# A kernel's first token tile takes its first product in plain float32 from unrounded weights, under a new order of work

## The chip, the cores and the metric

The kernel runs on one core of one Trainium2 chip. The metric is the device time of one execution in microseconds, as the median of several runs.

## The reference

```python
def _attn_ref(r, k, v, w, u):            # r, k, v: (4, 8, 768, 48); w, u: (8, 48)
    ...
    for t in range(S):
        kt, vt, rt = (k[:, :, t], v[:, :, t], r[:, :, t])
        cur = np.einsum('bhd,bhe->bhde', u[None] * kt, vt)
        y[:, :, t] = np.einsum('bhd,bhde->bhe', rt, state + cur)
        state = w[None, :, :, None] * state + np.einsum('bhd,bhe->bhde', kt, vt)

def _moe_ref(x, w_in, w_out, a, b):      # x: (3072, 384), w_in: (384, 2048), w_out: (2048, 384)
    h = x @ w_in
    h2 = h * h
    h3 = h2 * h
    P = a[0] + a[1] * h + a[2] * h2 + a[3] * h3
    Q = 1.0 + np.abs(b[0]) * np.abs(h) + np.abs(b[1]) * h2
    g = P / (Q + 1e-06)
    return (g @ w_out).astype(np.float32)
```

The attention's output y, with its heads side by side, is the x of the second function. The weights w_in and w_out come as float64, all else as float32.

## The kernel before

**Attention.** The 3072 tokens make 24 blocks of 128; the loads (kh, rh, vn) and the matmuls work on blocks or on pairs m of two blocks (12 pairs). For a block, kh and rh are scaled by powers of the decay (L633, L637), r times k is formed for the term in u (L641, into a tile m), multiplied by u (L646), reduced (L651, dt) and multiplied by v (L655). PE transposes kh and rh (tk and tr, L660), copies bring them to SBUF as kt and ys (L549, a helper `copy` that all engines' copies go through), a products (L682) are masked on DVE (L696), kv products (L712) carry the state, which DVE adds into vs (L725) and decays (L745), and y products (L736) give the result, added to m (L741). PE transposes m to x (L753). There are 7 tiles m.

**Two products.** A token tile f is two blocks (256 tokens; 12 tiles). x is copied to its rounded float32r half xth, and a subtraction gives the remainder xtl (L765). The 2048 columns of w_in are 16 groups j of 128. A slice s is two groups of one tile: 8 slices a tile, 97 in all, since the last one is halved. For one slice PE takes the first product f1 (`mm`, L775): for each j three row chunks, each by three float32r products of 256 columns (rounded weight by xth, rounded weight by xtl, remainder of weight by xth). Then the rational function: on ACT L817, L823, L828, L833 (ln, into z) and L837 (exp); on DVE u3 (L841), the rounded half of g (L847), p (L851), d (L857) and the remainder of g (L861, on DVE for slices 0 to 19, on POOL from 20 on). The second product f2 (`mm2`, L779 to L781) takes three float32r products of 384 columns for each j and block.

**Weights.** They come in 28 pieces, 12 of w_in (128x512) and 16 of w_out (128x384), each a float64 read as pairs of integers. A piece is loaded on SP's queue, and then goes from engine to engine: `cv_exp` on ACT (L516), `cv_shift` on DVE (L522), `cv_up` and `cv_sign` on ACT (L503, L507), for every fourth piece `cv_or` on DVE (L535) instead, `cv_round` on POOL (L540). The float32 piece that results (bits) is split: the rounded half (`cv_hi`, L549, on ACT or DVE) and the remainder (`cv_lo`, L546, on DVE or POOL). Four constant tiles keep halves and remainders: wi_hi, wi_lo, wo_hi, wo_lo.

**Order.** The kernel lists its steps as tasks with an engine or a choice of two, a cost, dependencies and buffers. `order_of` is a planner that runs when the kernel is built: it gives each task a key (from the tables AT for the pairs, CT for the pieces, OFF for the kinds of step), places the tasks on engines and returns one list, and the program is emitted in that order. Each engine then works through its own part strictly in order. Between the first rounds of work the planner puts matmuls on constants, called warm (L1096, bf16, 128x128), up to the first f2. After the last slices a flag decides whether a general form of the whole runs; in these runs it does not.

The first product in x and the second are float32r. The attention's products a, kv and y, and `us` (L401: one row of weights by 384 columns, in the preparation of the tables), are plain float32; the trace has two records for one such product.

Of the kernel before, what the change touches and what calls it, by code (L numbers as in the profile page):

```python
# [31 lines left out]
PRM = {'AT': (7.27, 41.94, 71.38, 117.31, 149.61, 223.87, 236.91, 267.74, 286.41, 287.5, 376.53, 394.8),  # L32
# [6 lines left out]
 'DUE': 7.86,  # L39
 'DX': 2.27,  # L40
 'FULL': (),
 'HFREE': 1,
# [4 lines left out]
 'OFF': {'LV': 249.97,
         'Lk': 358.43,
         'Lr': -577.02,
         'Lv': -349.7,  # L50
# [1168 lines left out]
```

## Time and profile before

| | |
|---|---|
| median of three runs | 562.29 us (561.52 to 562.76) |
| the profiled execution | 562.68 us, span 560.9 us |
| PE busy | 533.8 us (95%) |
| DVE busy | 464.8 us (83%) |
| ACT busy | 424.0 us (76%) |
| POOL busy | 267.4 us (48%) |
| mean granted clock of TensorE | 0.99 |

PE is the TensorE's matmul, PEld its weight loads, DVE the VectorE, ACT the ScalarE, POOL the GpSimd and SP the SyncE, whose queue issues the loads. The span is the time from the first to the last instruction of the profile; the execution's own time contains 1.8 us more. A line such as L775 is a line of the kernel, and out<-in are the tiles by name. A word in brackets behind a row of a timeline is the idle time that the engine had ahead of it, and whose work ended that. Durations of matmuls overlap: what one costs is the distance between two starts.

### The profile page before, as it was taken

To read this page: it belongs to the slowest core of one execution; us is meant where nothing else is said; L and a number is where in the kernel's file an instruction comes from. 1 tells how busy PE (TensorE), PEld (TensorE's weight loads), DVE (VectorE), ACT (ScalarE), POOL (GpSimd) and SP (SyncE) were. 2 spreads that over 40 slices of the span, in tenths; PEclk is the share of its full clock that TensorE was granted. 3 is DMA by queue.
4 is the path that set the end of the run, shared out by engine and by line. 5 is a ranking of instruction groups with operands and counts; after the bars stand their busy time and mean duration, and the time that the engine had idled before them with its cause. 6 is when DMAs were issued, how large, how long until landed. Compare 5 with 4: busy or idle time off the path is not lost.

```text
span 560.9 us, 14727 instructions
## 1 busy us (share of the span) xinstructions
PE 533.8 (95%) x5968; PEld 518.2 (92%) x5968; DVE 464.8 (83%) x738; ACT 424.0 (76%) x707; POOL 267.4 (48%) x260
## 2 busy tenths in 40 slices
PE   7899867699999999999999999999999999999996
PEld 6799756699998999988999999999999999999996
DVE  4887999999999776998799989668888977776773
ACT  6759887998776788965766767778878676888781
POOL 6688677671041223795569423327633312223221
PEclk9999979899999999999999999999999999999999
DMA  8556386503200006065133203003300000000001
GB/s 202 168 157 168 115 188 174 135 22 71 57 16 16 2 27 123 5 132 109 28 68 87 41 2 85 16 1 88 63 30 15 1 30 2 0 30 1 30 1 34
DMA packets 100032, 35.64 MB, mean 64 GB/s; under 512 B 93298, under 2 KB 96372, under 8 KB 99956
## 3 DMA queue, kind: packets, MB, share of 16 engines
q1 hardware_dynamic: 99956, 34.62, 25.7%
q8 instruction: 49, 0.80, 0.6%
q14 instruction: 27, 0.22, 0.1%
HBM read 29.89 MB, written 4.72 MB: 62 GB/s over the span
## 4 chain that ended last, share of the span: by engine, by line
PE 71%; DVE 17%; ACT 6%; issue 3%; POOL 2%; DVEq 0%; ACTq 0%; POOLq 0%
PE h L775 30%; PE o L779 10%; PE o L781 10%; PE o L780 10%; PE warm L1096 3%; PE y L736 3%; DVE g L847 2%; DVE q L851 2%; DVE vs L725 2%; DVE ys L696 1%; DVE h L841 1%; PE x L753 1%; DVE ys L549 1%; PE tr L660 1%; DVE h L857 1%
## 5 line engine op out<-in xcount | busy, mean ns | idle before, releaser
L861 POOL TENSOR_TENSOR g<-q,z 128x512 fp32r<-128x512 f32 (+1 forms) x77 | 99.1, 1287 | 188.6 <-DVE q L857 162.1
L775 PE MATMUL h<-xth,wi_hi 128*128 128x256 f32 x576 | 164.1, 285 | 1.8 <-DVE wi_hi L549 1.8
L775 PE MATMUL h<-xth,wi_lo 128*128 128x256 f32 x576 | 161.7, 281 | 0.9 <-POOL wi_lo L546 0.9
L775 PE MATMUL h<-xtl,wi_hi 128*128 128x256 f32 x576 | 161.5, 280 | 0.0
L779 PE MATMUL o<-wo_hi,g 128*128 128x384 f32 x384 | 134.5, 350 | 0.0
L781 PE MATMUL o<-wo_hi,g 128*128 128x384 f32 x384 | 130.4, 340 | 2.1 <-DVE g L861 2.1
L780 PE MATMUL o<-wo_lo,g 128*128 128x384 f32 x384 | 130.1, 339 | 0.0
L817 ACT ACTIVATE q<-h 128x512 f32<-128x512 f32 (+1 forms) x97 | 57.3, 591 | 81.0 <-PE h L775 78.3
L847 DVE SCALAR_TENSOR_TENSOR g<-h,sig,z 128x512 fp32r<-128x512 f32 (+1 forms) x97 | 72.1, 743 | 49.7 <-ACT z L837 46.9
L775 PEld LDWEIGHTS h<-xth,wi_hi 128*128 128x128 f32 x576 | 108.7, 189 | 2.5 <-DVE wi_hi L549 2.0
L775 PEld LDWEIGHTS h<-xth,wi_lo 128*128 128x128 f32 x576 | 108.7, 189 | 1.1 <-POOL wi_lo L546 1.1
L775 PEld LDWEIGHTS h<-xtl,wi_hi 128*128 128x128 f32 x576 | 108.8, 189 | 0.0
L841 DVE SCALAR_TENSOR_TENSOR h<-t,sig,h 128x512 f32<-128x512 f32 (+1 forms) x97 | 72.1, 744 | 7.7 <-ACT t L828 7.1
L851 DVE SCALAR_TENSOR_TENSOR q<-w,sig,g 128x512 f32<-128x512 f32 (+1 forms) x97 | 72.1, 743 | 5.1
L781 PEld LDWEIGHTS o<-wo_hi,g 128*128 128x128 f32 x384 | 72.6, 189 | 3.2 <-DVE g L861 3.2
L823 ACT ACTIVATE w<-q,off,root 128x512 f32<-128x512 f32 (+1 forms) x97 | 75.5, 779 | 0.0
L828 ACT ACTIVATE t<-h,off,root 128x512 f32<-128x512 f32 (+1 forms) x97 | 74.5, 769 | 0.1
L779 PEld LDWEIGHTS o<-wo_hi,g 128*128 128x128 f32 x384 | 72.7, 189 | 0.7
L780 PEld LDWEIGHTS o<-wo_lo,g 128*128 128x128 f32 x384 | 72.7, 189 | 0.0
L837 ACT ACTIVATE z<-z,lnb 128x512 f32<-128x512 f32 (+1 forms) x97 | 69.7, 718 | 2.4
L833 ACT ACTIVATE z<-w,lnb 128x512 f32<-128x512 f32 (+1 forms) x97 | 66.3, 683 | 3.1 <-DVE g L861 0.6
L857 DVE SCALAR_TENSOR_TENSOR q<-h,sig,q 128x512 f32<-128x512 f32 (+1 forms) x77 | 57.1, 741 | 1.9
(275 smaller groups left out, 804.4 us busy)
## 6 DMA issues: line engine op xcount, KB each, us to landing
sti<-in_moe_w_in_dram SPq DMA_DIRECT2D x12, 512.0 KB, 4.6
sto<-in_moe_w_out_dram SPq DMA_DIRECT2D x16, 384.0 KB, 3.4
rh<-in_r_dram SPq DMA_DIRECT2D x24, 192.0 KB, 3.5
vn<-in_v_dram SPq DMA_DIRECT2D x24, 192.0 KB, 3.6
kh<-in_k_dram SPq DMA_DIRECT2D x24, 192.0 KB, 3.3
out_dram<-os SPq DMA_DIRECT2D x24, 192.0 KB, 1.9
vs<-in_v_dram SPq DMA_DIRECT2D x32, 96.0 KB, 3.7
wraw<-in_w_dram SPq DMA_DIRECT2D x1, 1.5 KB, 2.2
```

What stands on the lines that cost most here:

```text
L775: nc.tensor.matmul(o, wt_[:, cc, ts(j, P)], x_[:, cc], start=(n == 0), stop=(n == 3 * NCC - 1))
L779: nc.tensor.matmul(o, hi, wo_hi[:, j], start=first, stop=False)
L780: nc.tensor.matmul(o, hi, wo_lo[:, j], start=False, stop=False)
L781: nc.tensor.matmul(o, lo, wo_hi[:, j], start=False, stop=last)
L823: nc.scalar.activation(g["w"], w_, AF.Square, scale=RB, bias=KB)
L828: nc.scalar.activation(g["t"], g["h"], AF.Square, scale=RA, bias=KA)
L833: nc.scalar.activation(g["z"], g["w"], AF.Ln, scale=2.0 ** -LN_SHIFT, bias=lnb[:, 2:3])
L837: nc.scalar.activation(g["z"], g["z"], AF.Exp, scale=-1.0, bias=lnb[:, 1:2])
L841: nc.vector.scalar_tensor_tensor(g["h"], g["t"], KAP, g["h"], op0=ALU.add, op1=ALU.mult)
L847: nc.vector.scalar_tensor_tensor(g["hi"], g["h"], c0, g["z"], op0=ALU.add, op1=ALU.mult)
L851: nc.vector.scalar_tensor_tensor(g["q"], g.get("w", g["q"]), qe, g["hi"].bitcast(F32), op0=ALU.add, op1=ALU.mult)
L861: e.tensor_mul(g["lo"], g["d"], g["z"])
```

## The change

Three things change together.

**Tile 0 in plain float32.** For the tiles in FULL (only tile 0, slices 0 to 7) f1 is `mm_full`: three plain float32 products for each j, of the unrounded piece f by an unrounded x. 144 float32r products become 48 plain ones. xth of tile 0 is float32, and it has no xtl. The first product of tile 0 depends on the piece's `cv_round` instead of its remainder; halves and remainders of w_in are needed from tile 1 on, and the remainder of a w_in piece is made after the last plain product that reads it.

**Buffers.** The pieces no longer have a place in four constant tiles. f, hi and lo of each are tiles of their own, from two rings ("wi" with 25 tiles, "wo" with 33), in which a piece's remainder takes the place of an f that has served. The z tiles ("tb") go from 3 to 2, since the conversions no longer use them, and the m tiles from 7 to 6.

**The order.** All tables of the planner have new numbers, halves and remainders have a table of their own (CS), and some costs differ. So nearly all steps stand elsewhere.

```diff
- 'FULL': (),
+ 'FULL': (0,),
...
- 'OFF': {'LV': 249.97,
...
+ 'OFF': {'LV': 270.26,
...
-    NM = 7
+    NM = 6
+    NTB = 2
+    NWI = FF // CW * NCC * 2 + 1
+    NWO = NJ * 2 + 1
...
-    wi_hi = cst.tile([P, NCC, FF], F32R, name="wi_hi")
-    wi_lo = cst.tile([P, NCC, FF], F32R, name="wi_lo")
-    wo_hi = cst.tile([P, NJ, DM], F32R, name="wo_hi")
-    wo_lo = cst.tile([P, NJ, DM], F32R, name="wo_lo")
...
+    def win(cc, j):
+        return pieces[(CW // P + NCC) * (j // (CW // P)) + cc], ts(j % (CW // P), P)
...
+    def cv_tile(c, nm, dt):
+        tag, bufs = ("wo", NWO) if c["n"] == DM else ("wi", NWI)
+        c[nm] = cst.tile([P, c["n"]], dt, tag=tag, name=f"w{nm}{c['nm']}", bufs=bufs)
+        return c[nm]
...
     def cv_hi(c, e):
-        copy(e, c["hi"], c["f"])
+        copy(e, cv_tile(c, "hi", F32R), c["f"])
...
-            xts[f] = tuple(at.tile([P, NCC, N1], F32R, tag=s, name=f"{s}{f}") for s in ("xth", "xtl"))
+            xts[f] = tuple(
+                at.tile([P, NCC, N1], F32 if f in FULL else F32R, tag=s, name=f"{s}{f}") for s in (("xth",) if f in FULL else ("xth", "xtl"))
+            )
...
-            for wt_, x_ in ((wi_hi, hi), (wi_hi, lo), (wi_lo, hi)):
-                nc.tensor.matmul(o, wt_[:, cc, ts(j, P)], x_[:, cc], start=(n == 0), stop=(n == 3 * NCC - 1))
+            w_, c = win(cc, j)
+            for nm, x_ in (("hi", hi), ("hi", lo), ("lo", hi)):
+                nc.tensor.matmul(o, w_[nm][:, c], x_[:, cc], start=(n == 0), stop=(n == 3 * NCC - 1))
                 n += 1
 
+    def mm_full(o, j, x_):
+        for cc in range(NCC):
+            w_, c = win(cc, j)
+            nc.tensor.matmul(o, w_["f"][:, c], x_[:, cc], start=(cc == 0), stop=(cc == NCC - 1))
...
-        mm(hps[s][:, ts(jj, N1)], j0 + jj, *xts[f])
+        (mm_full if f in FULL else mm)(hps[s][:, ts(jj, N1)], j0 + jj, *xts[f])
...
-        g["z"] = ew_tile(s, "tb", "z")
+        g["z"] = ew_tile(s, "tb", "z", bufs=NTB)
...
-            add(("co", p), lambda e, c=c, p=p: cv_lo(c, e), t + 3, {"D": 0.07 + 0.53 * x, "G": 0.15 + 1.07 * x}, [("ch", p)], use=[("bits", p)])
+            add(("co", p), lambda e, c=c, p=p: cv_lo(c, e), t + 1, {"D": 0.07 + 0.53 * x, "G": 0.15 + 1.07 * x}, [("ch", p), *last_use(p)], new=[(tag, ("wl", p))], use=[("wf", p)])
...
+            xin, win = ("xh", "cr") if full else ("xl", "co")
...
-                    deps + [("co", p0 + cc) for cc in range(NCC)], new=[] if jj else [("h", h)], use=[("xt", f)] + ([h] if jj else []), cols=2304)
+                    deps + [(win, p0 + cc) for cc in range(NCC)], new=[] if jj else [("h", h)], use=[("xt", f)] + ([h] if jj else []) + used([p0 + cc for cc in range(NCC)], s, full), cols=3072 if full else 2304)
```

Three places of the order follow, before and then now. Behind a name stands the number of the tile that the program gave it: the 0 in h0 is the slice, the 2 in tr2 and kh2 the block, and wfi0_1 is the plain piece f of w_in, column group 0, chunk 1; wloo1 is the remainder of the w_out piece 1.

PE, the first rows of slice 0's first product, before:

```order
L775 MATMUL h0_902<-xth0_825,wi_hi_103 128x256
L775 MATMUL h0_902<-xtl0_826,wi_hi_103 128x256
L775 MATMUL h0_902<-xth0_825,wi_lo_104 128x256
L775 MATMUL h0_902<-xth0_825,wi_hi_103 128x256
L775 MATMUL h0_902<-xtl0_826,wi_hi_103 128x256
L775 MATMUL h0_902<-xth0_825,wi_lo_104 128x256
```

PE, the same place now:

```order
L790 MATMUL h0_851<-xth0_807,wfi0_0_632 128x256
L790 MATMUL h0_851<-xth0_807,wfi0_1_217 128x256
L790 MATMUL h0_851<-xth0_807,wfi0_2_242 128x256
L667 MATMUL tr2_863<-identw_80,rh0_105 112x128 x4
L790 MATMUL h0_851<-xth0_807,wfi0_0_632 128x256
L790 MATMUL h0_851<-xth0_807,wfi0_1_217 128x256
L790 MATMUL h0_851<-xth0_807,wfi0_2_242 128x256
L790 MATMUL h1_882<-xth0_807,wfi0_0_632 128x256
```

Each j was nine products and is three, and the transposes tr2 of the second pair stand between the first j's products.

DVE, around tile 0's copy of x and the first product, before:

```order
L549 CAST xth0_825<-x0_814 128x3x128
L745 TENSOR_TENSOR vs0_107<-vs0_107,w128_93 48x384
L522 TENSOR_SCALAR bitso3_849<-cp6_834 128x384
L765 TENSOR_TENSOR xtl0_826<-x0_814,xth0_825 128x3x128
L765 TENSOR_TENSOR xtl0_826<-x1_843,xth0_825 128x3x128
L522 TENSOR_SCALAR bitsi1_2_918<-cp9_912 128x512
L546 TENSOR_TENSOR wo_lo_106<-bitso9_785,wo_hi_105 128x384
L522 TENSOR_SCALAR bitso4_946<-cp10_929 128x384
L633 TENSOR_TENSOR kh2_113<-kh2_113,wkn_92 128x8x48
L549 COPY kt_114<-tk2_979 112x512
L549 COPY ys0_115<-tr2_1026 48x512
L549 COPY ys1_116<-tr2_1026 48x512
```

DVE, the same place now:

```order
L556 COPY xth0_807<-x1_824 128x3x128
L640 TENSOR_TENSOR kh2_109<-kh2_109,wkn_92 128x8x48
L644 TENSOR_TENSOR rh0_105<-rh0_105,wrn_91 128x8x48
L553 TENSOR_TENSOR wloo1_861<-wfo1_798,whio1_858 128x384
L648 TENSOR_TENSOR m2_868<-rh0_105,kh2_109 128x384
L556 COPY ys0_111<-tr2_863 48x512
L653 TENSOR_TENSOR m2_868<-m2_868,ub_85 128x384
L529 TENSOR_SCALAR wfi3_2_886<-cp23_876 128x512
L658 TENSOR_REDUCE dt2_895<-m2_868 128x8
L662 TENSOR_TENSOR m2_868<-vn2_782,dt2_895 128x384
L856 SCALAR_TENSOR_TENSOR h0_851<-t0_893,sig_100,h0_851 128x512
L529 TENSOR_SCALAR wfo3_909<-cp6_904 128x384
```

The remainders xtl0 are gone, the copies of block 2's transposes stood behind four conversion steps and now stand behind one, and slice 0's u3 (L856 now) comes in the same dozen.

DVE, between the remainder of slice 14 and the steps of slices 15 and 16, before:

```order
L861 TENSOR_TENSOR g14_2468<-h14_2370,z14_2420 128x512
L841 SCALAR_TENSOR_TENSOR h15_2458<-t15_2492,sig_100,h15_2458 128x512
L696 TENSOR_TENSOR ys1_116<-a(3, 1)_2423,mask_81 64x8x64
L847 SCALAR_TENSOR_TENSOR g15_2533<-h15_2458,sig_100,z15_2505 128x512
L851 SCALAR_TENSOR_TENSOR q15_2488<-w15_2502,sig_100,g15_2533 128x512
L857 SCALAR_TENSOR_TENSOR h15_2458<-h15_2458,sig_100,q15_2488 128x512
L741 TENSOR_TENSOR m6_2139<-y6_2538,m6_2139 128x384
L861 TENSOR_TENSOR g15_2533<-h15_2458,z15_2505 128x512
L841 SCALAR_TENSOR_TENSOR h16_2510<-t16_2558,sig_100,h16_2510 128x512
L741 TENSOR_TENSOR m7_2196<-y7_2561,m7_2196 128x384
```

DVE, the same place now:

```order
L732 TENSOR_TENSOR vs0_103<-kv4_0_2415,vs0_103 48x384
L876 TENSOR_TENSOR g14_2404<-h14_2280,z14_2377 128x512
L732 TENSOR_TENSOR vs0_103<-kv4_0_2415,vs0_103 48x384
L732 TENSOR_TENSOR vs0_103<-kv4_1_2416,vs0_103 48x384 x2
L703 TENSOR_TENSOR ys0_111<-a4_0_2450,mask_81 64x8x64 x2
L703 TENSOR_TENSOR ys1_112<-a4_1_2451,mask_81 64x8x64 x2
L658 TENSOR_REDUCE dt10_2548<-m10_2498 128x8
L662 TENSOR_TENSOR m10_2498<-vn10_2256,dt10_2548 128x384
L648 TENSOR_TENSOR m11_2592<-rh1_107,kh2_109 128x384
L748 TENSOR_TENSOR m8_2165<-y8_2553,m8_2165 128x384
L856 SCALAR_TENSOR_TENSOR h15_2506<-t15_2570,sig_100,h15_2506 128x512
L748 TENSOR_TENSOR m9_2293<-y9_2575,m9_2293 128x384
```

Adds, masks and reduces of pairs 4 and 5 stand ahead of slice 15's u3, where one mask stood behind it before.

More of the change, by code (lines that the diff above doesn't have):

```diff
@@ new lines @@
+ 'OFF': {'LV': 270.26,
+         'Lk': 774.15,
+         'Lr': -796.68,
+         'Lv': -312.07,
+         'a': -341.47,
+         'ae': 398.71,
+         'ba': 33.75,
+         'bb': -348.95,
+         'beta': -354.71,
+         'bs': -201.32,
+         'bv': -386.72,
+         'c0': -322.33,
+         'c2': 127.85,
+         'c3': -103.81,
+         'ca': -140.2,
+         'ch': 121.32,
+         'cl': -34.78,
+         'cl_': -128.33,
+         'co': -647.77,
+         'coef': 293.84,
+         'cr': 213.5,
+         'cs': -175.01,
+         'ctr': -337.17,
+         'cu': -134.42,
+         'd': -35.41,
+         'ex': -222.41,
+         'f1': -18.42,
+         'f2': 29.16,
+         'flag': -59.53,
+         'flagm': 645.83,
+         'flagt': 524.35,
+         'hi': 12.18,
+         'id': 91.47,
+         'inv': -624.91,
+         'kv': 150.51,
+         'kve': -232.22,
+         'ln': 63.38,
+         'lo': -1043.9,
+         'msk': 27.33,
+         'od': 129.99,
+         'os': -15.92,
+         'p': 68.22,
+         'pad': 25.39,
+         'pl': 54.79,
+         'pow': -277.52,
+         'q': 362.68,
+         'rest': 10.15,
+         'sk': 150.8,
+         'sq': -301.08,
+         'sr': -807.06,
+         'st0': 436.05,
+         't': 292.34,
+         'tab': -679.44,
+         'tk': 221.19,
+         'tke': 109.8,
+         'tr': -205.98,
+         'tre': 482.82,
+         'turn': -129.33,
+         'u3': -36.29,
+         'ub': 38.7,
+         'ube': -359.69,
+         'ubp': -906.35,
+         'uw': -294.57,
+         'w': -428.73,
+         'w128': -805.12,
+         'wl': 257.36,
+         'wp': 221.72,
+         'x': -170.77,
+         'xh': 511.5,
+         'xl': 55.87,
+         'y': -297.22,
+         'ye': 218.13,
+         'z': 276.11},
@@ L124 @@
  'WARM0': 1.6,
- 'WARM1': 260.37,
- 'X': (49.3, 8.02, 7.96, 3.84)}
+ 'WARM1': 732.75,
+ 'X': (52.55, 30.05, 13.36, 10.85),
+ 'FULL2': (),
+ 'FINE': {}}
 ENGINES = "PDAGS"
@@ L555, in tile_linear_attention_rational_ffn @@
         for cc in range(NCC):
-            piece(wi_hi[:, cc, ts(g, CW)], wi_lo[:, cc, ts(g, CW)], wi32[ts(cc, P), ts(g, 2 * CW)], CW, f"i{g}_{cc}")
+            piece(wi32[ts(cc, P), ts(g, 2 * CW)], CW, f"i{g}_{cc}")
         for j in range(g * (CW // P), (g + 1) * (CW // P)):
-            piece(wo_hi[:, j, :], wo_lo[:, j, :], wo32[ts(j, P), :], DM, f"o{j}")
+            piece(wo32[ts(j, P), :], DM, f"o{j}")
     TR = HALF + D
@@ L888, in f2 @@
             c = ds(jj * N1 + hf * P, P)
+            if f in FULL2:
+                w_, o = wout(j0 + jj), ops[f][hf][:, 0:DM]
+                nc.tensor.matmul(o, gs[s]["hi"][:, c].bitcast(F32), w_["f"], start=opens(s) and jj == 0, stop=False)
+                nc.tensor.matmul(o, gs[s]["lo"][:, c], w_["hi"], start=False, stop=closes(s) and jj == nj - 1)
+                continue
             mm2(
@@ L939, in add, with last_use @@
             tags[buf] = tag
+    def last_use(p):
+        g, k = divmod(p, NCC + CW // P)
+        if k < NCC:
+            us = [("f1", s, jj) for s, (f, j0, nj) in enumerate(SL) for jj in range(nj) if f in FULL and (j0 + jj) // 4 == g]
+        else:
+            us = [("f2", s, 1) for s, (f, j0, nj) in enumerate(SL) if f in FULL2 and j0 <= 4 * g + k - NCC < j0 + nj]
+        return us[-1:]
     def build():
@@ L1008, in build, with used @@
                 add(("xh", n), lambda e, n=n: xt_hi(n, e), due(m) + 13, {"A": 0.37, "D": 0.47}, [("x", n)], use=[("x", n), ("xt", m)])
-                add(("xl", n), lambda e, n=n: xt_lo(n), due(m) + 14, {"D": 0.47}, [("xh", n)], use=[("x", n), ("xt", m), ("m", n)])
-        lastf = {SL[s][0]: s for s in range(NS)}
+                if m not in FULL:
+                    add(("xl", n), lambda e, n=n: xt_lo(n), due(m) + 14, {"D": 0.47}, [("xh", n)], use=[("x", n), ("xt", m), ("m", n)])
+        def used(ps, s, full):
+            return [(nm, p) for p in ps for nm in (("wf",) if full else ())]
+        keep = [(nm, p) for nm in ("wh", "wl") for p in range(len(pieces))]
         for s in range(NS):
```

157 lines of the change are left out of this document (44 added, 113 removed), and 12 rows, old and new, of the table PRM.

## Prediction

> **What bounds the kernel now.** I read the page's head and its chain first, then a table of stretches, then single rows where one engine waits. From the page: the span, the busy line, and the chain that ended last by engine.
>
> ```profile
> span 560.9 us, 14727 instructions
> PE 533.8 (95%) x5968; PEld 518.2 (92%) x5968; DVE 464.8 (83%) x738; ACT 424.0 (76%) x707; POOL 267.4 (48%) x260
> PE 71%; DVE 17%; ACT 6%; issue 3%; POOL 2%; DVEq 0%; ACTq 0%; POOLq 0%
> ```
>
> PE is busy for 95% of the span, but 17% of the chain is DVE. The stretches tell where. Columns: the stretch in us, its length, busy time and instructions of PE, PEld, DVE, ACT and POOL, granted clock, DMA share, GB/s.
>
> ```profile
> core 0: us, PE busy (x) PEld busy (x) DVE busy (x) ACT busy (x) POOL busy (x), PEclk, DMA share, GB/s
> 0.00:17.00 17.00, 13.69 (x159) 12.42 (x160) 8.51 (x18) 12.24 (x24) 9.91 (x25) 1.00 0.87 222
> 17.00:40.00 23.00, 20.67 (x461) 19.67 (x458) 21.86 (x50) 14.74 (x31) 17.69 (x17) 1.00 0.47 135
> 40.00:56.00 16.00, 16.00 (x234) 15.91 (x232) 11.54 (x17) 14.47 (x28) 13.91 (x14) 1.00 0.73 177
> 56.00:117.00 61.00, 47.33 (x619) 42.18 (x617) 58.16 (x97) 51.97 (x96) 42.77 (x41) 0.92 0.56 142
> 117.00:157.30 40.30, 40.27 (x450) 39.22 (x449) 38.36 (x59) 33.14 (x55) 11.44 (x13) 1.00 0.24 50
> 157.30:185.00 27.70, 26.83 (x354) 25.71 (x354) 26.27 (x42) 19.20 (x33) 9.65 (x11) 1.00 0.05 16
> 300.00:549.00 249.00, 248.97 (x2403) 246.10 (x2400) 199.89 (x308) 190.36 (x304) 95.15 (x82) 1.00 0.12 28
> ```
>
> From 117 us on PE has next to no gap (0.03 in 40.3 us, 0.9 in 27.7, 0.03 in 249). Its work there is fixed, so the end moves with the time at which PE becomes full. From 56 to 117 PE is idle for 13.7 us, at a mean granted clock of 0.92, while DVE is idle for only 2.8: tile 0's slices with the conversions and attention beside them are bound by DVE. Before 56 us DVE's idle time is 8.5 (0 to 17), 1.1 (17 to 40) and 4.5 us (40 to 56). The marks 56.0 and 117.0 are the ends of the elementwise step d (L857) of slices 0 and 6, 157.3 is that of slice 15. In DVE's timeline (start, duration, line, operation, the wait ahead in brackets):
>
> ```profile
> 39.34 1.00 DVE L765 TENSOR_TENSOR xtl<-x,xth 128x384 fp32r<-128x384 f32 x2
> ...
> 41.21 0.69 DVE L522 TENSOR_SCALAR bitsi<-cp 128x512 int32<-128x512 int32 x1 [0.87 <-ACT cp L516]
> 42.57 0.81 DVE L546 TENSOR_TENSOR wo_lo<-bitso,wo_hi 128x384 fp32r<-128x384 f32 x1 [0.66 <-ACT wo_hi L549]
> 46.20 0.69 DVE L549 COPY kt<-tk 112x512 f32<-112x512 f32 x1 [1.18 <-PE tk L660]
> 48.43 1.39 DVE L549 COPY ys<-tr 48x512 f32<-48x512 f32 x2 [1.53 <-PE tr L660]
> 55.22 0.75 DVE L857 SCALAR_TENSOR_TENSOR h<-h,sig,q 128x512 f32<-128x512 f32 x1
> 116.21 0.75 DVE L857 SCALAR_TENSOR_TENSOR h<-h,sig,q 128x512 f32<-128x512 f32 x1
> 157.65 0.68 DVE L861 TENSOR_TENSOR g<-h,z 128x512 fp32r<-128x512 f32 x1
> ```
>
> The four waits (0.87, 0.66, 1.18, 1.53) are 4.2 of the 4.5 us that DVE stands idle from 40 to 56: DVE is waiting for a conversion and for the second pair's transposes. PE's timeline has the first product, the first second product and that of slice 15:
>
> ```profile
> 40.95 0.36 PE L775 MATMUL h<-xth,wi_hi 128*128 128x256 f32 x1
> 56.16 0.42 PE L779 MATMUL o<-wo_hi,g 128*128 128x384 f32 x1
> 163.18 0.42 PE L779 MATMUL o<-wo_hi,g 128*128 128x384 f32 x1
> ```
>
> Slice 15's remainder ends on DVE at 158.3 and PE takes it at 163.2: DVE is ahead of PE by 4.9 us there.
>
> **The plain product on PE.** Removed are 144 rounded products of 256 columns (16 column groups j by 9), added 48 plain ones. The price of the rounded ones comes from the chain late in the run, where 18 of them (two j) are one row:
>
> ```profile
> 504.89 2.12 PE h L775 x18
> 11.95 0.91 PE L401 MATMUL us<-ur,ones 1*128 1x384 f32 x2
> 12.79 0.79 PE L1096 MATMUL warm<-wones 128*128 128x128 bf16 x11
> ```
>
> And from the groups of PE between 117 and 165 us (count, busy us, mean ns):
>
> ```profile
> L736 PE MATMUL y<-vs,ys 128*64 128x48 f32 x64 | 2.1, 223 | 0.0
> ```
>
> So nine cost 1.06 us, one 0.118. No 128-row plain product of this size is in the trace. The nearest is L401 (plain float32, 384 columns, one row of weights): one matmul in the program, two records in the trace, and PE takes the next work 0.84 us after it began. Scaled to 256 columns that is 0.56, by three 1.68 per j, and 16 x (1.68 - 1.06) = +9.9 us of PE. The y products are plain float32 too, with 48 columns and two records each: 64 records, 32 products, in 2.1 us (L736), or 0.066 each. Scaled to 256 columns this is 0.35 if they go one by one, 0.70 if the two halves of the array's columns work side by side. So the ends are 16 x (3 x 0.35 - 1.06) = -0.2 and 16 x (3 x 0.70 - 1.06) = +16.6 us. I take L401's +9.9, as it alone has a product that fills all 128 output rows. Nearly all of it falls into the stretch with 13.7 us of PE idle and costs the end nothing: 3.8 us of cover are left. If the cover were gone, the excess (2.9 at the upper end) would come straight on the end. [...]
>
> Latency: the first slice's product lengthens by 1.2 us (two j by 0.62) ahead of ACT's chain. But it starts earlier: it no longer waits for rounded halves and remainders, nor for xt's remainders (the two L765 at 39.34). I count the net as nothing, because DVE has conversions queued beside it.
>
> **DVE up to slice 0.** In the order DVE has 83 instructions up to d of slice 0 before, 84 after; kind by kind the work differs by 0.2 us. So what moves d0 is the idle time, 14.1 us. The change puts the second pair's transposes and the scaling that feeds them around the first product, and DVE copies ys0 from tr2 five instructions behind xt's copy where it was ten behind; two of the four waits (1.18 + 1.53) go, and the conversions' two (0.87 + 0.66) mostly, as fewer rounds through ACT stand there. What is late next is the chain z to exp on ACT, which has 9 instructions more in front of its exp of slice 0; by the table it was idle for 14.6 us there. I take -3.5 us. The ends: 0 (the waits come back in other places) and -9 (all but some 5 us that the loads at the start impose, by the 8.5 us of idle time in the first 17).
>
> **DVE from slice 0 to slice 6.** 96 instructions before, 89 after. Prices from the groups of DVE (count, busy us, mean ns):
>
> ```profile
> L549 DVE CAST wo_hi<-bitso 128x384 fp32r<-128x384 f32 x5 | 1.8, 356 | 0.5 <-POOL bitso L540 0.4
> L549 DVE CAST wi_hi<-bitsi 128x512 fp32r<-128x512 f32 x4 | 1.8, 456 | 0.1
> L765 DVE TENSOR_TENSOR xtl<-x,xth 128x384 fp32r<-128x384 f32 x24 | 13.1, 551 | 1.4 <-ACT xth L549 1.1
> L546 DVE TENSOR_TENSOR wo_lo<-bitso,wo_hi 128x384 fp32r<-128x384 f32 x6 | 5.3, 876 | 0.8 <-ACT wo_hi L549 0.7
> L646 DVE TENSOR_TENSOR m<-m,ub 128x384 f32<-128x384 f32 x6 | 5.0, 830 | 0.1
> L741 DVE TENSOR_TENSOR m<-y,m 128x384 f32<-128x384 f32 x24 | 13.0, 550 | 1.9 <-PE y L736 1.9
> L651 DVE TENSOR_REDUCE dt<-m 128x8 f32<-128x384 f32 x24 | 13.0, 546 | 0.3
> L696 DVE TENSOR_TENSOR ys<-a(3, 0)_2422,mask 64x512 f32<-64x512 f32 x2 | 1.4, 690 | 0.1
> ```
>
> Counted from the start to d6: rounded halves 9 to 3 (four of 0.36 and two of 0.46: -2.3), xt remainders 5 to 2 (-1.7), m times u 3 to 1 (-1.7), w_out remainders 6 to 5 (-0.9), w_in remainders 2 to 4 (+1.4, 0.68 each as slice 15's g, a subtraction of the same size), r times k 0 to 3 (+1.7, 0.55 as L741), and ten others of both signs (about +0.1). The sum is -3.4 by means. Since neighbours overlap by some 0.1 us, I take **-2.8**. The rounded halves go to ACT (19 to 25) and remainders partly stay on POOL (20 to 19). ACT gets 1.5 us more up to exp of slice 6, and has 9.0 us idle in that stretch; POOL has 18.2. If ACT's idle time were spent in waits, up to that 1.5 would come back: it is inside the range.
>
> **Slices 7 to 15: a debt that falls due.** From d6 to d15 the new order gives DVE four masks (2.8), four adds of kv (2.2), four reduces (2.2), four adds of y (2.2) more, with eight others net +3.6: 13.0 us. The price is from L696, L651 and L741. Pair 4 and half of pair 5 come earlier. PE gets its own part of it there: one pair's y (32 products), two pairs' a, 24 transposes, three of xt, about 7.0 us. From the same groups of PE (117 to 165 us):
>
> ```profile
> L682 PE MATMUL a(3, 0)_2422<-ys,kt 48*64 48x64 f32 x32 | 1.2, 221 | 0.0
> L660 PE MATMUL tr<-identw,rh 128*112 128x128 f32 x16 | 2.5, 276 | 0.0
> ```
>
> (2.0 for y; 1.2 for one pair's a, whose two halves run interleaved in that time, so 2.4; 2.5 for 16 transposes holds the pipeline's end of each four, without it some 0.4 for four, so 2.4; 0.2 for xt.) So DVE loses 13.0 - 7.0 = 6.0 us against PE. Its cover is the 4.9 us of lead, and some of the 1.9 us of its own idle time from 117 to 157.3: PE waits for 1.1 us or less. The same sum to slice 19 (DVE 9, PE 6) gives nothing more, so I take **+1.0**; ends 0 (the idle time covers the rest) and +6.0 (no lead).
>
> **What costs nothing.** 103 warm matmuls go: they only fill PE's waits ahead of the first second product. The loads are the same 28 of weights, and kh2 and rh0 move by one place on SP's queue. Two z buffers instead of three: the ln of slice s+2 starts only after the remainder of s has ended, by 0.2 us at the closest place I see:
>
> ```profile
> 214.65 1.29 POOL L861 TENSOR_TENSOR g<-q,z 128x512 fp32r<-128x512 f32 x1 [2.49 <-PE o L781]
> 216.13 0.69 ACT L833 ACTIVATE z<-w,lnb 128x512 f32<-128x512 f32 x1
> ```
>
> If that were short, ACT would wait by tenths of a microsecond while PE has later slices in hand. Six m tiles instead of seven can hold attention's next pair back, but behind 117 us that stands beside full PE. Behind slice 19 the amount of work is that of before.
>
> **Sum.** -3.5 - 2.8 + 1.0 = -5.3. The profiled execution took 562.7 us (span 560.9 and 1.8 around it), so 557.4; the median of the runs, 562.3, lies 0.4 below it, so **557.0 us**. With all ends on one side: 550.5 (-9 - 2.8 + 0) and 568.4 (0 - 2.8 + 6.0 + 2.9).
>
> **Rivals.** 0.2% of this kernel (1.1 us: 561.2 to 563.4) is about what a measurement can tell from no change.
> - Forecast, 0.60, own range 554.5 to 560.5: PE full at about 111 instead of 117, a short wait at slice 15.
> - Larger gain, 0.15: idle time ahead of d0 falls by 7 or more and slice 15 is covered: 562.3 - 7 - 2.8 = 552.5 to 555. For it: loads end early (DMA share 0.47 in 17 to 40). Against it: 8.5 of the idle time lies in the first 17 us, which the change hardly touches.
> - Same, 0.12: DVE's idle time only moves, and the 2.8 saved are given back by slice 15: about 561.5 to 562. For it: DVE's work to d0 is unchanged. A plain product at the upper price ends here too: 557.0 + 2.9, and the rest by the granted clock of 0.92, which makes PE's work in that stretch longer.
> - Slower, 0.13: the debt on DVE at slice 15. Without the lead of 4.9 us PE waits for 6.0; with no gain ahead of d0 that is 562.3 - 2.8 + 6.0 = 565.5. It decides where the two front gains together are below the wait. For it: PE becomes full earlier and so comes to slice 15 earlier, which eats DVE's lead. Against it: the lead is made by the earlier d6 as well, as both engines move together.
>
> The range 552.5 to 563.0 holds the forecast, the larger gain and the same case; the slower case is left out.
>
> **What would show it.** Right: the first plain product at 36 to 39 us, d of slice 0 at 50 to 53, the first second product right behind, d of slice 6 near 111, PE without gaps from there, and a PE wait of one to two us for DVE's g between slices 13 and 19. Three plain products of a j take between 1.4 and 1.7. Wrong: DVE idle by over 4 us between the first product and d0 (the waits came back); PE full but d6 no earlier (plain products became the bound); or waits of over 3 us for g at slices 7 to 19 (the debt).

## Result and profile after

The changed kernel takes 556.44 us in the median of five runs (555.81 to 559.07), the kernel before 562.54 us beside it (561.52 to 563.26). The ratio is 0.990, with a 95% interval from 0.9873 to 0.9926: 6.1 us faster, where 557.0 us was forecast. The profiled execution took 556.55 us. From the head of its page:

```profile
span 554.6 us, 14472 instructions
PE 528.4 (95%) x5817; PEld 509.6 (92%) x5817; DVE 465.9 (84%) x736; ACT 427.8 (77%) x714; POOL 262.9 (47%) x255
PE 68%; DVE 20%; ACT 6%; issue 3%; POOL 1%; DMA 1%; SPq 0%; DVEq 0%; ACTq 0%; POOLq 0%
```

The shares hardly move; the stages do. Below are the stretches that answer to those of before, cut at the ends of d of slices 0, 6 and 15 (53.3, 111.3 and 161.9 us). First the kernel before up to slice 0, which had been shown in three parts, then the changed kernel.

```profile
0.00:56.00 56.00, 50.36 (x846) 48.00 (x847) 41.91 (x83) 41.46 (x81) 41.50 (x54) 1.00 0.66 174
```

```profile
0.00:53.30 53.30, 45.80 (x709) 41.97 (x710) 44.45 (x84) 43.24 (x84) 36.82 (x50) 1.00 0.69 187
53.30:111.30 58.00, 47.84 (x604) 41.81 (x602) 55.05 (x89) 52.20 (x100) 43.90 (x41) 0.97 0.53 139
111.30:161.90 50.60, 50.36 (x688) 47.90 (x687) 49.50 (x81) 41.16 (x71) 30.39 (x33) 1.00 0.37 76
161.90:187.60 25.70, 25.22 (x340) 24.31 (x339) 24.74 (x40) 18.21 (x29) 1.65 (x2) 1.00 0.29 63
300.00:542.60 242.60, 240.49 (x2314) 237.09 (x2313) 196.53 (x300) 182.96 (x291) 92.82 (x79) 1.00 0.12 27
```

Slice 0's d ends 2.7 us earlier, the way from there to slice 6 is 3.0 us shorter (58.0 for 61.0), and so PE is full 5.7 us earlier. DVE is busy for 95% of that second stretch in both kernels (58.16 of 61.0, 55.05 of 58.0). Behind slice 6 the span gains another 0.6 us (443.9 us from there to the end before, 443.3 now). The span is 6.3 us shorter in all.

The marks in the timelines of PE and DVE are the first plain product, the first second product (L794), and d of slices 0 and 6:

```profile
38.61 1.53 PE L790 MATMUL h<-xth,wfi 128*128 128x256 f32 x6
54.71 0.42 PE L794 MATMUL o<-whio,g 128*128 128x384 f32 x1
```

```profile
52.55 0.74 DVE L872 SCALAR_TENSOR_TENSOR h<-h,sig,q 128x512 f32<-128x512 f32 x1
110.55 0.75 DVE L872 SCALAR_TENSOR_TENSOR h<-h,sig,q 128x512 f32<-128x512 f32 x1
```

The waits of PE from slice 6 to the end, the longest groups first:

```profile
PE tk L667 <- DVE xtl L774: 2.1, 1, 2.1
PE y L743 <- DVE ys L703: 0.6, 1, 0.6
PE y L743 <- DVE vs L732: 0.5, 1, 0.5
PE kv L719 <- ACT ys L556: 0.2, 1, 0.2
```

None is for g, the wait that the prediction had expected near slice 15. Instead there is one of 2.1 us for xtl, far behind, at 412 us.

### The profile page after: what moved, and what is told of

It is laid out like the page before. It is cut to its first block, busy times and chain, and to the rows that moved or that the text cites. A ratio compares the mean times of both kernels' runs of the same rounds, so it can differ in the third digit from the quotient of the medians.

```text
span 554.6 us, 14472 instructions
## 1 busy us (share of the span) xinstructions
PE 528.4 (95%) x5817; PEld 509.6 (92%) x5817; DVE 465.9 (84%) x736; ACT 427.8 (77%) x714; POOL 262.9 (47%) x255
## 4 chain that ended last, share of the span: by engine, by line
PE 68%; DVE 20%; ACT 6%; issue 3%; POOL 1%; DMA 1%; SPq 0%; DVEq 0%; ACTq 0%; POOLq 0%
PE h L784 28%; PE o L794 10%; PE o L796 9%; PE o L795 9%; PE warm L1135 3%; DVE ys L703 3%; PE y L743 3%; DVE g L862 2%; DVE h L856 2%; DVE q L866 2%; DVE vs L732 2%; DVE h L872 1%; PE a L689 1%; PE x L760 1%; DVE ys L556 1%
## 5 line engine op out<-in xcount | busy, mean ns | idle before, releaser
L784 PE MATMUL h<-xth,whii 128*128 128x256 f32 x528 | 150.2, 284 | 0.0
L784 PE MATMUL h<-xth,wloi 128*128 128x256 f32 x528 | 147.5, 279 | 0.0
L784 PE MATMUL h<-xtl,whii 128*128 128x256 f32 x528 | 147.4, 279 | 0.0
L794 PE MATMUL o<-whio,g 128*128 128x384 f32 x384 | 134.7, 351 | 0.0
L795 PE MATMUL o<-wloo,g 128*128 128x384 f32 x384 | 130.1, 339 | 2.9 <-DVE wloo L553 2.9
L796 PE MATMUL o<-whio,g 128*128 128x384 f32 x384 | 130.2, 339 | 1.0 <-DVE g L876 1.0
L784 PEld LDWEIGHTS h<-xth,whii 128*128 128x128 f32 x528 | 99.3, 188 | 0.6
L784 PEld LDWEIGHTS h<-xtl,whii 128*128 128x128 f32 x528 | 99.3, 188 | 0.0
L784 PEld LDWEIGHTS h<-xth,wloi 128*128 128x128 f32 x528 | 99.2, 188 | 0.0
L856 DVE SCALAR_TENSOR_TENSOR h<-t,sig,h 128x512 f32<-128x512 f32 (+1 forms) x97 | 72.0, 743 | 7.4 <-ACT t L843 7.0
L795 PEld LDWEIGHTS o<-wloo,g 128*128 128x128 f32 x384 | 72.8, 190 | 3.5 <-DVE wloo L553 3.4
L796 PEld LDWEIGHTS o<-whio,g 128*128 128x128 f32 x384 | 72.6, 189 | 1.9 <-DVE g L876 1.9
L794 PEld LDWEIGHTS o<-whio,g 128*128 128x128 f32 x384 | 72.6, 189 | 1.1 <-ACT whio L556 0.2
```

The source lines that it names most:

```text
L784: nc.tensor.matmul(o, w_[nm][:, c], x_[:, cc], start=(n == 0), stop=(n == 3 * NCC - 1))
L794: nc.tensor.matmul(o, hi, w_["hi"], start=first, stop=False)
L795: nc.tensor.matmul(o, hi, w_["lo"], start=False, stop=False)
L796: nc.tensor.matmul(o, lo, w_["hi"], start=False, stop=last)
L856: nc.vector.scalar_tensor_tensor(g["h"], g["t"], KAP, g["h"], op0=ALU.add, op1=ALU.mult)
```

## The experiments

The theory going in, called the cover theory: the plain products cost the end nothing as long as PE has idle time, and the end moves with DVE's time up to slice 6. Its rivals: the plain products themselves bring the gain (product theory), the new numbers of the planner bring it alone (order theory), and later PE and its clock.

**The two halves of the change, each alone.** The changed kernel with its new tables but without a plain tile:

```diff
- 'FULL': (0,),
+ 'FULL': (),
```

> The changed kernel's code and tables, but no tile in plain float32 (FULL empty), so the planner lists the steps anew and tile 0 needs rounded halves and remainders again. Cover theory (the end moves with DVE's time to slice 6, which the plain products shorten by making halves and remainders of w_in later): 560 to 565 us. Order theory (the new tables alone bring the gain): 555.5 to 558. Product theory (any order gains by the plain products and loses them here): near 562.5.

Measured: 571.87 us, ratio 1.0166 (1.0152 to 1.0179). The other half: the changed kernel's code, with the old tables.

```diff
-PRM = {'AT': (12.19, 36.51, 65.8, 109.86, 123.26, 133.52, 193.98, 232.99, 282.09, 313.75, 378.77, 401.82),
...
+PRM = {'AT': (7.27, 41.94, 71.38, 117.31, 149.61, 223.87, 236.91, 267.74, 286.41, 287.5, 376.53, 394.8),
...
+ 'FULL': (0,),
...
+PRM['CS'] = tuple(t + 2.5 for t in PRM['CT'])
```

> The changed kernel's code with the old tables of numbers (CS set to the old CT plus 2.5, the rule that it had before) and tile 0 in plain float32. Cover theory: DVE gets rid of some halves and remainders but the order isn't fitted to it: 558 to 563 us. Product theory: 556 to 559. Order theory: 561.5 to 563.5.

Measured: 565.68 us, ratio 1.0057 (1.004 to 1.0073). Neither half is faster than the kernel before: only the two together gain. Order theory and product theory fall. But both results lie above every range given, that of the cover theory too (by 6.9 and 2.7 us), so it does not explain them either. Their stretches from the start to d0 and from d0 to d6, first of the new tables without plain products, then the second stretch of the old tables with them:

```profile
0.00:63.60 63.60, 54.34 (x899) 51.29 (x900) 52.37 (x93) 48.70 (x94) 48.54 (x58) 0.95 0.67 171
63.60:119.60 56.00, 42.89 (x589) 39.54 (x587) 51.41 (x84) 43.05 (x80) 39.81 (x39) 0.88 0.56 139
```

```profile
51.30:116.60 65.30, 51.70 (x608) 44.81 (x605) 59.04 (x101) 57.34 (x107) 45.88 (x44) 0.92 0.55 138
```

With the new tables but rounded products DVE does 93 instructions ahead of d0 instead of 84, and d0 comes at 63.6 instead of 53.3. With the old tables and plain products d0 comes at 51.3, 4.7 us earlier than before, and all but 0.4 of it is gone at d6 (116.6), since DVE has 101 instructions in between and stands idle for 6.3 us.

That is not the whole loss. From d6 to the end the kernel before takes 443.9 us, the new tables without plain products 451.4 and the old tables with them 447.4. So 7.5 us of the first kernel's longer span (10.1 us) and 3.5 us of the second's (3.1 us) lie behind d6. PE is not full there in either kernel: it is idle for 12.1 and 10.1 us, where it was for 7.8, and busy for 3.2 and 1.1 us more. With the old tables its longest wait stands right behind d6, for the remainder of a g:

```profile
117.75 0.69 PE L797 MATMUL o<-whio,g 128*128 128x384 f32 x1 [3.48 <-DVE g L877]
```

The end moves with d6 only where the order behind it keeps PE full.

**The exchange on PE alone, in the old order.** The kernel before, with three plain products for nine in tile 0, on the rounded halves:

```diff
-        mm(hps[s][:, ts(jj, N1)], j0 + jj, *xts[f])
+        (mm_full if f == 0 else mm)(hps[s][:, ts(jj, N1)], j0 + jj, *xts[f])
...
+    def mm_full(o, j, hi, lo):
+        for cc in range(NCC):
+            nc.tensor.matmul(o, wi_hi[:, cc, ts(j, P)].bitcast(F32), hi[:, cc].bitcast(F32), start=(cc == 0), stop=(cc == NCC - 1))
```

> The kernel before in its own order, with three plain float32 products in place of nine rounded ones for each j of tile 0. They read the rounded halves of w_in and x, so the part of the remainders in tile 0 is left out; all conversions stay where they are. It shows what the exchange on PE alone does. PE has 16 x (1.30 - 1.06) = 3.8 us more by the changed kernel's trace (two j, 12 records, in 2.60 us). Cover theory: hidden in PE's idle time, 561.5 to 563.5 us. Product theory: 560 or less. If plain products are on the path: 564 to 566.5.

Measured: 563.06 us, ratio 1.0011 (1.0000 to 1.0022). As the cover theory has it: in the old order the exchange on PE by itself is worth nothing.

**How much cover there is.** Every plain product twice:

```diff
-            nc.tensor.matmul(o, w_["f"][:, c], x_[:, cc], start=(cc == 0), stop=(cc == NCC - 1))
+            nc.tensor.matmul(o, w_["f"][:, c], x_[:, cc], start=(cc == 0), stop=False)
+            nc.tensor.matmul(o, w_["f"][:, c], x_[:, cc], start=False, stop=(cc == NCC - 1))
```

> The changed kernel in its own order with every plain product of tile 0 issued twice (so tile 0's first product comes out doubled). PE gets 16 x 1.30 = 20.8 us more. Cover theory: PE's idle time of 1.8 us (37 to 53.3) and 10.2 us (53.3 to 111.3) takes 12 of it at most, the rest is on the end: 563 to 568 us. If all of it is on the path: 577. If none: 556.5.

Measured: 571.29 us, 14.9 above the changed kernel for some 20.8 us of added work, outside the range. From d0 to d6:

```profile
56.80:123.40 66.60, 61.35 (x669) 55.30 (x667) 56.74 (x90) 53.07 (x99) 44.62 (x41) 0.95 0.47 121
```

PE still stands idle for 5.2 us in a stretch in which it is now the busiest engine, and its list of waits there has three, all for DVE (2.9, 1.9 and 0.5 us). Idle time of PE is thus not all cover: part of it lies where PE waits for DVE, and more work did not fit in there. About 6 us were covered, half of the 12 that I had added up from the idle time. (Of the 14.9 us, 1.0 stands in the trace by 21 us already, ahead of the first plain product; the last section shows from what.)

**Less work for PE.** One of three plain products:

```diff
-            nc.tensor.matmul(o, w_["f"][:, c], x_[:, cc], start=(cc == 0), stop=(cc == NCC - 1))
+            if cc == 0:
+                nc.tensor.matmul(o, w_["f"][:, c], x_[:, cc], start=True, stop=True)
```

> The changed kernel in its own order, with one of the three plain products of each j of tile 0 (row chunk 0 alone, so the other two thirds of tile 0's first product are left out). PE gets 32 x 0.433 = 13.9 us less. Cover theory as predicted (plain products beside PE's idle time, DVE is the bound): 555.5 to 556.5 us. If PE is a bound beside DVE, as the 14.9 us of 20.8 that doubled products cost suggest: 549 to 554 us. Issue less by 13.9 on the end: 542.5.

Measured: 560.3 us, slower than the changed kernel by 3.9 with 13.9 us less work: a miss of all three expectations. The stretch from 50 to 120 us of both, the changed kernel first (the third number from the end is PE's mean granted clock):

```profile
50.00:120.00 70.00, 59.57 (x707) 53.21 (x708) 66.94 (x110) 63.62 (x119) 52.52 (x49) 0.98 0.45 118
```

```profile
50.00:120.00 70.00, 53.65 (x629) 48.11 (x630) 64.55 (x103) 60.12 (x113) 51.64 (x49) 0.80 0.46 118
```

PE, now less busy, is granted 0.80 of its clock instead of 0.98 over 70 us, and d0 to d6 takes 60.5 us instead of 58.0. Attention's y and kv products take 278 and 279 ns by their means there, where they took 224 and 207. From d0 to d6 the changed kernel's list has no wait of DVE for PE; this kernel's has three:

```profile
DVE ys L703 <- PE a L689: 0.9, 1, 0.9
DVE vs L752 <- PE y L743: 0.7, 1, 0.7
DVE vs L732 <- PE kv L719: 0.3, 1, 0.3
```

Whether the clock is the cause was tried by filling the place of the two missing products with bf16 products on constants:

```diff
             if cc == 0:
+                for _ in range(15):
+                    nc.tensor.matmul(o[:, 0:P], wones, wones, start=True, stop=True)
                 nc.tensor.matmul(o, w_["f"][:, c], x_[:, cc], start=True, stop=True)
```

> The kernel with one of three plain products for each j of tile 0 (the other two thirds of that product left out, as in plain_third), and 15 bf16 matmuls of 128 columns on constants in their place (about 0.87 us, the time of the two plain ones), overwritten by the product. If plain_third lost its 3.9 us to the lower granted clock of a PE that is less busy: 556 to 557.5 us, and the clock from 50 to 120 us as in the changed kernel. If it lost them by another cause (earlier products crowd ACT or DVE): about 560.

Measured: 558.26 us, between the two expectations. Its stretches from d0 to d6 and from 50 to 120 us:

```profile
54.60:112.70 58.10, 48.85 (x737) 42.77 (x735) 55.12 (x90) 52.46 (x100) 44.11 (x42) 0.94 0.53 139
50.00:120.00 70.00, 59.53 (x836) 52.97 (x834) 66.95 (x108) 63.76 (x119) 53.00 (x50) 0.95 0.48 123
```

d0 to d6 is back at 58.1 us, and DVE's three waits for PE are gone from the list: work without any use gave the 2.5 us back. The fill also puts the remaining product of each j back to about its old place, so the run does not separate the clock from that; the slower products and DVE's waits for them speak for the clock. The 1.8 us left are not in this stretch: d0 comes 1.3 later than in the changed kernel, all of it there by 21 us and so ahead of tile 0's first product, and near 410 us the clock drops.

**The same filling in the old order.** The changed kernel has a higher clock from 50 to 120 us than the kernel before (0.98 against 0.93), so part of its gain could be the clock.

```diff
+        if 1 <= s < 8:
+            for _ in range(10):
+                nc.tensor.matmul(hps[s][:, ds(jj * N1, P)], wones, wones, start=True, stop=True)
         mm(hps[s][:, ts(jj, N1)], j0 + jj, *xts[f])
```

> The kernel before, in its own order, with 10 bf16 matmuls of 128 columns on constants ahead of each j's first product in slices 1 to 7 (140 in all, about 8.1 us of the 13.7 us that PE is idle there). Clock theory (half of the change's gain is that PE, busier with plain products, keeps its clock: the mean deficit from 50 to 120 us is 5.2 us before and 1.7 after): 558.5 to 561. Cover theory (DVE's time alone counts): 562 to 563.5. If the fill gets in the way of products: 564 to 570.

Measured: 563.57 us, ratio 1.001 (1.0001 to 1.0019). No gain: the fill raised the clock there only to 0.95, and DVE's stretch from d0 to d6 stayed at 61.4 us. In the old order the clock is not what holds DVE up. That the clock has no share in the gain is not shown by this, as the fill didn't reach 0.98. The share can hardly be large: in the kernel before, DVE is idle for 2.8 us from d0 to d6, and its list of waits there has one for PE, of 0.3 us.

**DVE's time, put back.** Reductions whose result nobody uses, at three places of the changed kernel's own order; this is `more`:

```diff
+    def more(n):
+        for _ in range(n):
+            nc.vector.tensor_reduce(scratch, ub, axis=mybir.AxisListType.X, op=ALU.add)
...
+        more(6 if s == 0 else 0)               # dve_first: behind u3
+        more(1 if s in range(6) else 0)        # dve_early: behind d
+        more(2 if s in range(9, 15) else 0)    # dve_late: behind d
```

> The changed kernel in its own order, with six more reductions of 384 columns (0.46 us from start to start, 2.8 us in all; their result is not used) on DVE right behind slice 0's u3. Cover theory (DVE's time up to slice 6 is on the path): 558.5 to 559.5 us, all of it but what falls into the 1.5 us of DVE's idle time between 37 and 53.3. If slice 0 waits for ACT or PE and not for DVE: 556.5.

Measured: 560.34 us, 3.9 above the changed kernel and 0.8 above the range. d0 ends at 56.3, 3.0 later, and d6 at 114.0, 2.7 later; another 1.3 us come behind d6, with the clock at 0.84 from 410 to 420 us. But 1.0 us of the 3.0 is there by 21 us, long ahead of the edit. And the six reductions, back to back, take 3.4 us (46.70 to 50.10) and not 2.8. Of these, 0.3 fill idle time behind u3, and 1.1 come back as two remainders of w_in get shorter (2.38 us to 1.28; the last section shows from what). What is left of the 3.4, 2.0 us, is what the edit itself adds to d0: one for one.

> The changed kernel in its own order, with one such reduction behind d of each of slices 0 to 5 (six, 2.8 us). This gives DVE back the 2.8 us that the prediction said it saves there. Cover theory: 558.5 to 559.5 us. If PE with its plain products is the bound there instead: 556 to 557.

Measured: 559.44 us, 3.0 above and inside the cover theory's range, but by luck. d0 comes 1.0 later though the edit stands behind it (again by 21 us), d0 to d6 takes 58.7 us, 0.7 more than in the changed kernel, and the rest lies behind d6, with PE's clock at 0.83 from 410 to 420. Of the dose of 2.8 us DVE's busy time shows 1.2 (56.27 for 55.05), as two remainders of w_in fell from 1.04 and 1.50 us to 0.68 each; 0.5 went into idle time. It was repeated in a larger dose (below).

> The changed kernel in its own order, with two such reductions behind d of each of slices 9 to 14 (twelve, 5.5 us). DVE's lead on PE at slice 15 is 2.7 us in the changed kernel's trace, and its idle time from slice 6 to slice 15 is 1.1 us. Cover theory: 558 to 559.5 us (5.5 less 2.7, less up to 1.1). If DVE is the bound there: 562. If PE is full and the lead comes back: 556.5.

Measured: 564.85 us, 8.4 above, outside every range. d of slice 6 is 1.7 us late already, ahead of the edit (1.2 of it by 21 us). A pair of reductions takes 1.05 us from its start to the next instruction's, so the dose is 6.3 us and not 5.5. From d6 to d15:

```profile
113.00:170.50 57.50, 52.04 (x688) 49.37 (x687) 55.54 (x94) 41.32 (x71) 30.40 (x33) 0.97 0.33 67
```

57.5 us instead of 50.6, or 6.9 for 6.3 us of work, with PE idle for 5.5 and its clock at 0.97. DVE's lead of 2.7 us at slice 15 absorbed none of it.

**The wait at 412 us.** PE waits there for xtl of tile 9. DVE's timeline shows the block that forms the flag ahead of it, 4.0 us long, with these as its first steps, and PE's the wait:

```profile
406.07 0.54 DVE L467 TENSOR_TENSOR okw<-wraw,wcol 128x3 f32<-128x3 f32 x1
406.53 0.15 DVE L471 TENSOR_TENSOR ctmp<-cabs 128x1 f32<-128x1 f32 x1
...
```

```profile
412.58 0.65 PE L667 MATMUL tk<-identw,kh 128*112 128x128 f32 x4 [2.06 <-DVE xtl L774]
```

```diff
-        add(("flag",), lambda e: pro_flag(), 400, {"D": 2.0}, [("cl_",), ("sq",), ("lo", 2 * NS // 3)])
+        add(("flag",), lambda e: pro_flag(), 400, {"D": 2.0}, [("cl_",), ("sq",), ("lo", 84)])
```

> The changed kernel with one dependency moved: the block of small DVE steps that forms the flag (L467 to L480, 3.9 us in the trace) waits for slice 84 instead of slice 64, so it stands behind xtl of tiles 9 to 11. In the changed kernel PE waits 2.1 us for xtl of tile 9, which stands behind that block on DVE. If the block is the cause: 554 to 555 us and no lower clock near 410 us. If another wait takes its place: 556 to 557.

Measured: 555.41 us, ratio to the kernel before 0.987 (0.9852 to 0.9889); span 553.0. d of all slices up to 60 stands within 0.1 us of the changed kernel's, that of slice 80 is 2.2 us earlier (479.3 for 481.5), and the wait for xtl is 0.5 us:

```profile
409.02 0.41 PE L760 MATMUL x<-identw,m 128*128 128x128 f32 x2 [0.49 <-DVE xtl L774]
```

The block was the cause of that wait. The time lies 0.4 above the range for this case, as 0.5 us of a wait is left. This is the fastest version here: clearly faster than the kernel before, and 1.0 us below the changed kernel by medians. The two intervals overlap, so for this last microsecond there is only the pair of traces, equal up to slice 60 and 1.6 us apart in their spans.

**The larger dose on that version.** Two reductions behind d of each of slices 0 to 5:

```diff
+        more(2 if s in range(6) else 0)
```

> The kernel with the later flag (555.4 us) and two reductions of 384 columns behind d of each of slices 0 to 5 (twelve, 0.46 us each, 5.5 us in all). In its order PE no longer waits at 410 us, which blurred the run with six. If DVE's time from slice 0 to slice 6 is on the path one for one: 559.5 to 561 us (5.5 less at most 1.5 of the 3 us of DVE's idle time there). If it is shared (ACT, PE and DVE wait for one another, and six reductions moved d of slice 6 by only 0.7 us against d of slice 0): 556.5 to 558.5 us.

Measured: 561.17 us, 5.8 above its base and 0.2 above the range. At 1.05 us a pair the dose is 6.3 us. From d0 to d6, the base first:

```profile
53.30:111.30 58.00, 47.76 (x603) 41.73 (x601) 55.04 (x89) 52.21 (x99) 43.98 (x41) 0.97 0.54 139
53.50:117.90 64.40, 52.25 (x601) 45.54 (x599) 60.62 (x101) 53.41 (x101) 44.63 (x42) 0.87 0.48 125
```

6.4 us longer, with the clock at 0.87 instead of 0.97. DVE is busy for 5.6 us more (two remainders of w_in got shorter again, by 1.2 us together) and idle for 0.8 us more, so its idle time covered nothing. From d6 to the end it is 441.6 us, 441.7 in the base. So in this stretch DVE's time is on the path about one for one, and all of it is on the end. (How much of the 0.8 us is PE's lower clock is not shown; DVE's waits for PE there come to 0.2 us.)

## Why the prediction was right, point by point

The time, its direction and the place of the gain were right, and so was the mechanism up to d of slice 6. That the sum came so close is in part luck, as the first term was 0.8 us too large and the third 1.6 us off to the other side. The terms:

| term | forecast | measured |
|---|---|---|
| up to d of slice 0 | -3.5 | -2.7 |
| slice 0 to slice 6 | -2.8 | -3.0 |
| behind slice 6 | +1.0 | -0.6 |
| sum (span) | -5.3 | -6.3 |

- **What bounds the kernel.** Right: work added to DVE ahead of slice 6 is on the path (2.0 us net gave 2.0 at d0, 5.6 us gave 6.4 at d6 and 5.8 on the end). Where the order behind d6 stays, so does the time from there to the end: 443.9 us in the kernel before, 443.8 with the exchange on PE alone and 444.0 with the filling. It is a property of the order, though, and not of the kernel: both halves of the change alone lose 3.5 us or more there.
- **The price of a plain product.** Mis-sized. Forecast 0.56 us from L401; measured 0.433. The row from the chain of waits, for two j, which are six products (two records each):

```profile
87.78 2.60 PE h L790 x12
```

  1.30 us per j, below the 1.4 to 1.7 given, so +3.8 us for tile 0 and not +9.9. L401's distance to the next work, scaled by columns, was too dear; what else it holds is not shown. Since either price is covered, the sum didn't feel it.
- **Cover on PE.** Right in its verdict (the exchange in the old order: 563.06), wrong in its size: of 20.8 us more only some 6 were covered, where the idle time promised 12. At the forecast's own price of 0.56, which makes 6.1 us more than measured, that cover would have been about used up.
- **Up to slice 0.** The sign was right, and from 40 us on so was the step: DVE's idle time there fell from 4.5 to 1.0 us, the 3.5 forecast, and the two waits for transposes are gone. The term hides two errors beside it. Ahead of 40 us, which the forecast left as it was, idle time fell by another 1.8 us. And DVE's busy time rose from 41.9 to 44.5, with one instruction more, where I had put 0.2 us of change: I had counted equal kinds at equal prices. The 19 steps of one to three columns took 7.3 us where they had taken 5.6, and remainders of w_in cost more. From the groups of DVE, first these remainders up to slice 6 of the kernel before, then of the changed one:

```profile
L546 DVE TENSOR_TENSOR wi_lo<-bitsi,wi_hi 128x512 fp32r<-128x512 f32 x2 | 1.4, 688 | 2.6 <-ACT wi_hi L549 2.6
```

```profile
L553 DVE TENSOR_TENSOR wloi<-wfi,whii 128x512 fp32r<-128x512 f32 x4 | 4.9, 1248 | 0.0
```

  The same subtraction takes 1.25 us there instead of 0.69. No run was made for it, but the changed kernel's trace shows what such steps meet (last section): three of the four, of 1.77, 1.04 and 1.50 us, started 0.2 to 0.5 us behind a step of POOL that was still running; the fourth, 0.9 us behind one, took 0.69.
- **Slice 0 to slice 6.** Right by its count: 96 instructions to 89, DVE busy 58.16 to 55.05 us, the way shorter by 3.0.
- **The debt at slice 15.** It fell due without a wait: d15 came 4.6 us later than before while d6 was 5.7 earlier, and PE, which got its own part of pairs 4 and 5, was busy for 50.36 of 50.6 us. The failing step is the idea of a debt that a lead pays: 6.3 us more on DVE there cost 6.9, with a lead of 2.7 us in the trace. DVE (49.50 of 50.6) and PE are both full in that stretch, each in strict order, so what DVE is ahead by at one slice is not there at another. The order fits without slack; the sum of work told that, the lead did not. PE's work behind d6 was not fixed either: it is busy for 434.7 us from there to the end, where it was for 436.1, with 0.8 us more of idle time. That is the -0.6; where the 1.4 us of work went was not followed.
- **Not seen at all.** The 2.1 us wait for xtl at 412 us, and the clock: with 13.9 us less for PE the way from d0 to d6 took 60.5 us instead of 58.0, at a clock of 0.80 instead of 0.98 from 50 to 120 us. No rival named a lower clock as a price of less work on PE.
- **What costs nothing.** The fewer z and m tiles were not tried by themselves, so that they cost nothing stays an argument.

The larger-gain, same and slower rivals did not come. The forecast's marks came at 38.6 (36 to 39 forecast), 53.3 (50 to 53), 54.7 and 111.3 us (near 111). The wait for g that should have come with them did not.

## What to carry to other kernels

Where an engine off the end's path binds an early stage, count its instructions up to the mark at which the last engine becomes full, and price idle time and busy time apart. The mark then tells the end, as long as the order behind it keeps that engine full (here 443.8 to 444.0 us from d6 to the end in three kernels of one order). An idle engine is cover only where it doesn't wait for the very engine that binds (here some 6 us of 12). And a table of an order is tuned to one mix of work: the new step and the new order each lost alone (565.7 and 571.9 us) and won together, so test them as a pair, and read the waits of the result once more, as one dependency gave about another microsecond. When work is added as a test, take its dose and the start of the stretch from the run's own trace: 2.8 us by plan were 3.4, and a microsecond of the effect stood ahead of the edit.

## What the runs showed of the hardware that was not expected

- Less work on PE can cost time: 13.9 us less made the kernel 3.9 us slower, at a mean granted clock of 0.80 from 50 to 120 us instead of 0.98. Useless products in place of the missing ones brought the clock to 0.95 and d0 to d6 from 60.5 back to 58.1 us.
- The clock fell behind the wait for xtl (0.83 to 0.86 over 10 us, between 410 and 430 us) in the traces of four kernels, where PE waits for 2.0 to 2.4 us. It did not in three others with the same wait of 2.1 to 2.3 us, the changed kernel's own among them. A mean of 0.83 over 10 us would be 3.4 us at 0.50, an estimate, and in windows of one microsecond the clock reads 0.50 from 415 to 418 us in dve_early. So such a wait may or may not cost more: by the arithmetic 1.7 us, and in dve_first, dve_early and the kernel with one product and the fill the way from d6 to the end is 1.2 to 1.6 us longer than in the changed kernel.
- In these traces a step of DVE that starts while a step of POOL runs can end with it (0.99 and 0.98 us below, where another takes 0.15), and one of POOL that starts behind DVE's can take longer (1.44 us, where the same one takes 1.02). The changed kernel's DVE, then its POOL:

```profile
16.66 0.15 DVE L394 SCALAR_TENSOR_TENSOR off<-beta,pts 128x1 f32<-128x1 f32 x1
16.85 0.99 DVE L395 SCALAR_TENSOR_TENSOR off<-off,half 128x2 f32<-128x2 f32 x1
17.95 0.98 DVE L397 SCALAR_TENSOR_TENSOR sig<-coef,sig 128x1 f32<-128x1 f32 x1
```

```profile
16.81 1.02 POOL L640 TENSOR_TENSOR kh<-kh,wkn 128x384 f32<-128x384 f32 x1 [1.79 <-ACT wkn L460]
17.90 1.01 POOL L648 TENSOR_TENSOR m<-rh,kh 128x384 f32<-128x384 f32 x1
```

  Two steps of one or two columns that start 0.04 and 0.05 us behind POOL's take 0.99 and 0.98 us and end with it; the one that meets nothing takes 0.15. In the kernel with the larger dose DVE started first, with a remainder of w_in at its short time, and POOL's step took 1.44 us:

```profile
69.26 0.68 DVE L553 TENSOR_TENSOR wloi<-wfi,whii 128x512 fp32r<-128x512 f32 x1
69.37 1.44 POOL L640 TENSOR_TENSOR kh<-kh,wkn 128x384 f32<-128x384 f32 x1 [1.75 <-DMA kh<-in_k_dram]
```

  So the price of such a step went here with what the other engine ran at that moment: the step of L395 takes 0.99 us above, 0.04 behind POOL's start, and 0.16 us in the kernel with the larger dose, where it starts 0.01 ahead of POOL's (16.96 and 16.97 us). Which kinds of step hold each other was not tested.
- This also moved d of slice 0 by 1.0 to 1.3 us in five runs on the changed order (the first three with reductions, the doubled products, and one product with the fill), whatever their edit. POOL's step of 16.81 us starts there between 15.99 and 16.55, four of DVE's small steps meet a step of POOL instead of three, and DVE is 1.0 to 1.3 us late by 21 us. With one trace a kernel it is not shown how much of this the medians carry.
